# The softmax work of the later batches, cut into halves and spread over the steps of the main loop

## The chip, the cores and the metric

The kernel runs on one core of a Trainium2 chip. The metric is the device time of one execution in microseconds (us), the median of three runs. TensorE is called PE here, VectorE DVE, ScalarE ACT, GpSimd POOL and SyncE SP, as in the profile.

## What is computed

There are 8 batches, each with 8 heads, 576 tokens and 64 numbers a head. First 32 pack tokens attend to the keys and values of a batch; then the queries attend to the 32 packed results. What comes out, 4608 rows of 512 numbers, goes through a gated layer with 1536 inner columns.

```python
def sm_attn(qq, kk, vv):
    s = scale * np.matmul(qq, kk.transpose(0, 1, 3, 2))
    s = s - np.max(s, axis=-1, keepdims=True)
    a = np.exp(s)
    a = a / (np.sum(a, axis=-1, keepdims=True) + 1e-09)
    return np.matmul(a, vv)
p_packed = sm_attn(p, k, v)
attn = sm_attn(q, p_packed, p_packed)
# x: attn as rows of (token, head * 64)
g = x @ w_gate
silu = g * (1.0 / (1.0 + np.exp(-g)))
out = (silu * (x @ w_val)) @ w_out
```

## The kernel before

The packed result of a batch is multiplied with the weights of gate and value first (`m_part`, which leaves the high and low parts `mh` and `ml`), so that the second attention's weights (`a2h`, `a2l`) can be multiplied with that directly. Each operand of the large products is split into a rounded high part and a rest, and three products are summed.

The main loop runs over the batches b, and within one over 12 chunks of 128 inner columns (`fc`). In a chunk, `gv_chunk` makes the gate tile and the value tile for half A of the tokens (256 of them), then for half B (320). Each such half takes two PSUM banks of the tag `gv`, of which there are only two: the gate tile is read by the Silu on ACT (`sg`, L435), the value tile by `hf` and, for half B, by `t` as well (L438, L441, both on DVE). The next half's gate tile can be written once the Silu has read the last one, its value tile once `hf` and `t` have. `h_split` makes `hh` on ACT and `hl` on DVE; `out_mm` (L446), one chunk later, multiplies them with the output weights.

The attention of the next batch, d = b + 1, is made between these products: `aux_of(b)` is a generator, and `fill()` takes one step of it after every half chunk (from chunk 1 on; an `m_part` for the next two chunks stands in the odd chunks). PE's instructions stand in the order in which this code is written. The other engines' order is set by a scheduler that goes by the order of the code and by what depends on what; each engine then works through its own list from first to last. The products of the attention and of `m_part` use two PSUM banks of the tag `aux`; those of `m_part` come free when DVE has made `ml` (L85).

Batches 0 and 1 go over the older functions (`s1_...`); batches 2 to 7 take `q_scores` (L262), `q_weights` and `q_pack` (L325) for the pack tokens, where the tokens lie on the partitions by quarters and the heads by parity. In `q_weights` the sums over a quarter (L284) go to DRAM and come back for all four quarters (L287, L289); then follow the common factor (L295 to L306), the product of the weights with it (L307) and the transpositions (L312). All batches then take `s2_scores` (two groups of products, L164, and transpositions L348), `s2_max` (L363, L364), `s2_exp` (L368, on ACT), `s2_norm` (sum L375, L376, L377, scale L378) and `s2_back` (transposition L384 and the split into `a2h` and `a2l`). The argument `both` lets one instruction work on both halves of the tokens, 128x1152 numbers. The attention of batch 1 is made during batch 0, which keeps the values h of all chunks (`kept`, h0) and splits them only later; the output weights are converted there too (L101 to L105).

Of the kernel before, what the change touches and what calls it, by code (L numbers as in the profile page):

```python
# [15 lines left out]
ALU = mybir.AluOpType  # L16
AX = mybir.AxisListType
# [3 lines left out]
B, H, S, D = 8, 8, 576, 64  # L21
NP = 32
DM, DF = 512, 1536
P = 128
NPAR, NHP = 2, 4
NFC = DF // P
SC, NSC = 96, 6
NJ, SQ = 4, S // 4
# [13 lines left out]
def tile_pack_attention_swiglu(ctx: ExitStack, tc: tile.TileContext, qT, kT, v, vq, pT, wgv, wout, out):  # L42


    nc = tc.nc
# [37 lines left out]
    def split(dst_h, dst_l, src, hi=nc.scalar, lo=nc.vector):  # L83
        copy(hi, dst_h, src)
        lo.tensor_tensor(dst_l, src, dst_h.bitcast(F32), op=ALU.subtract)  # L85
# [52 lines left out]
    def load_k(b):  # L138
        p_t = pool.tile([P, NHP, NP], F32, tag="p", bufs=2, name="p_t")
        (nc.sync if b else nc.scalar).dma_start(p_t, pT[b])  # L140
        k_t = io_tile([P, 2, NHP, HS], F32, "k_t")
        for hf in range(2):
            nc.sync.dma_start(k_t[:, hf], kT[b, :, hf])
        kps[b] = (k_t, p_t)
# [21 lines left out]
    def s1_scores(b, direct):  # L166
        k_t, p_t = kps[b]
        t1 = pool.tile([P, NPAR, S], F32, tag="s2", bufs=1, name="t1")
        mx = pool.tile([P, NPAR, 2], F32, tag="mx1", bufs=2, name="mx1")
        nm = pool.tile([P, 2, NPAR], F32, tag="nm1", bufs=2, name="nm1")  # L170
        rs = pool.tile([P, 3, NPAR], F32, tag="rs1", bufs=3, name="rs1")
        st1[b] = [t1, rs, nm]
        kept = []
        for hf in range(2):
            pss = [ps(), ps()]
            kept.append(pss)
            by_head(
                [x[:, :HS] for x in pss], lambda r, hp: p_t[r, hp, :],
                lambda r, hp: k_t[r, hf, hp],
            )  # L180
            for par in range(NPAR):
                nc.vector.tensor_reduce(mx[:, par, hf : hf + 1], pss[par][:, :HS], axis=AX.X, op=ALU.max)
                if not direct:
                    nc.scalar.copy(t1[:, par, hf * HS : (hf + 1) * HS], pss[par][:, :HS])  # L184
            yield
        nc.vector.tensor_reduce(nm[:, 0], mx, axis=AX.X, op=ALU.max)
        nc.vector.tensor_scalar(nm[:, 1], nm[:, 0], -SCALE, None, op0=ALU.mult)
        if direct:
            for par in range(NPAR):
                for hf in range(2):  # L190
                    nc.scalar.activation(
                        t1[:, par, hf * HS : (hf + 1) * HS], kept[hf][par][:, :HS], AF.Exp,
                        bias=nm[:, 1, par : par + 1], scale=SCALE, accum_out=rs[:, 1 + hf, par : par + 1],
                    )
            nc.vector.tensor_tensor(rs[:, 0], rs[:, 1], rs[:, 2], op=ALU.add)

    def s1_exp(b):
        t1, rs, nm = st1[b]
        for par in range(NPAR):
            nc.scalar.activation(  # L200
                t1[:, par], t1[:, par], AF.Exp, bias=nm[:, 1, par : par + 1], scale=SCALE, accum_out=rs[:, 0, par : par + 1]
            )
# [74 lines left out]
    def q_weights(b):  # L277


        e, z = sq[b]  # L280
        ev = e.rearrange("p r h n -> p (r h) n")
        nc.scalar.activation(ev[:, :, :SQ], ev[:, :, :SQ], AF.Exp, scale=SCALE)
        zv = z.rearrange("p s r h -> p s (r h)")
        nc.vector.tensor_reduce(zv[:, 1], ev[:, :, :SQ], axis=AX.X, op=ALU.add)  # L284
        x = pool.tile([P, NJ, 2, H], F32, tag="x1", bufs=1, name="x1")
        zd = dram.tile([P, 2, H], F32, tag="zd", bufs=2, name="zd")
        nc.sync.dma_start(zd, zv)  # L287
        for i in range(NJ):
            nc.sync.dma_start(x[NP * i : NP * i + NP], zd.rearrange("(j n) s h -> n j s h", j=NJ))  # L289
        for _ in range(3):  # L290
            yield
        y = pool.tile([P, 3, NJ + 1, H], F32, tag="pp", bufs=1, name="y1")
        m, t, f = y[:, 2, 0], y[:, 2, 1], y[:, 2, 2]
        tc.keep_in_program_order(
            nc.vector.tensor_reduce(m, x[:, :, 0].rearrange("p j h -> p h j"), axis=AX.X, op=ALU.max)  # L295
        )
        nc.vector.tensor_tensor(
            y[:, 0, :NJ], x[:, :, 0], m.unsqueeze(1).broadcast_to([P, NJ, H]), op=ALU.subtract
        )
        nc.vector.tensor_tensor(y[:, 0, NJ], zv[:, 0], m, op=ALU.subtract)  # L300
        nc.scalar.activation(y[:, 0], y[:, 0], AF.Exp, scale=SCALE)
        nc.vector.tensor_tensor(y[:, 1, :NJ], y[:, 0, :NJ], x[:, :, 1], op=ALU.mult)
        nc.vector.tensor_reduce(t, y[:, 1, :NJ].rearrange("p j h -> p h j"), axis=AX.X, op=ALU.add)
        nc.vector.tensor_scalar(f, t, 1e-9, None, op0=ALU.add)
        nc.vector.reciprocal(t, f)
        nc.vector.tensor_tensor(f, t, y[:, 0, NJ], op=ALU.mult)  # L306
        nc.vector.tensor_tensor(  # L307
            ev[:, :, :SQ], ev[:, :, :SQ], f.unsqueeze(2).broadcast_to([P, H, SQ]), op=ALU.mult
        )
        a1 = pool.tile([P, NPAR, NHP, NKQ, NP], F32, tag="a1", bufs=1, name="a1")  # L310
        for par in range(NPAR):
            nc.vector.transpose(  # L312
                a1[:, par].rearrange("p h k n -> p (h k n)"), e[:, par].rearrange("p h n -> p (h n)")
            )
        sq[b] = a1
        for _ in range(2):
            yield

    def q_pack(b):
        a1, v_t = sq.pop(b), vs.pop(b)  # L320
# [11 lines left out]
    def s2_tiles(b):  # L332
        st2[b] = (
            pool.tile([P, 2, NPAR, HS], F32, tag="s2", bufs=1, name="s2"),
            pool.tile([P, 3, 2 * NPAR * NBK], F32, tag="r2", bufs=1, name="r2"),
        )
# [14 lines left out]
    def s2_view(b, cs):  # L351
        s2, r2 = st2[b]
        n = NPAR * NBK
        rows = slice(cs.start * n, cs.stop * n)
        return (
            s2[:, cs].rearrange("p c r (k n) -> p (c r k) n", n=NP),
            [r2[:, i, rows] for i in range(3)],
            [P, (cs.stop - cs.start) * n, NP],
        )

    def s2_max(b, cs):
        x, (m, _, _), shape = s2_view(b, cs)
        nc.vector.tensor_reduce(m, x, axis=AX.X, op=ALU.max)  # L363
        nc.vector.tensor_tensor(x, x, m.unsqueeze(2).broadcast_to(shape), op=ALU.subtract)  # L364
# [5 lines left out]
    def s2_a2(b):  # L370
        a2[b] = tuple(pool.tile([P, NPAR, S], F32R, tag=t, bufs=2, name=t) for t in ("a2h", "a2l"))

    def s2_norm(b, cs):
        x, (m, s, r), shape = s2_view(b, cs)
        nc.vector.tensor_reduce(s, x, axis=AX.X, op=ALU.add)  # L375
        nc.vector.tensor_scalar(m, s, 1e-9, None, op0=ALU.add)  # L376
        nc.vector.reciprocal(r, m)  # L377
        nc.vector.tensor_tensor(x, x, r.unsqueeze(2).broadcast_to(shape), op=ALU.mult)  # L378

    def s2_back(b, c):  # L380
        s2, _ = st2[b]
        ah, al = a2[b]
        t = pool.tile([P, NPAR, HS], F32, tag="t2", bufs=1, name="t2")
        nc.vector.transpose(t.rearrange("p r n -> p (r n)"), s2[:, c].rearrange("p r n -> p (r n)"))  # L384
        at = (slice(None), slice(None), slice(c * HS, (c + 1) * HS))
        split(ah[at], al[at], t)
# [72 lines left out]
    both = slice(0, 2)  # L459
# [6 lines left out]
    def aux_of(b):  # L466

        d = b + 1
        if d == B:
            return  # L470
        if d < NEARLY:
            yield from s1_scores(d, False)
            if d + 1 < B:
                load_k(d + 1)
            s1_exp(d)
            yield
            yield from s1_post(d)
        else:
            yield from q_scores(d)
            yield from q_weights(d)  # L480
            if d + 1 < B:
                load_k(d + 1)
            q_pack(d)
            yield
            yield
        if d + 1 < B:
            load_v(d + 1)
        s2_tiles(d)
        yield from s2_scores(d)
        if d + 1 < B:  # L490
            load_q(d + 1)
        s2_max(d, both)
        s2_exp(d, both)
        s2_norm(d, both)
        s2_a2(d)
        for c in range(2):
            s2_back(d, c)

    with tc.manual_schedule(engines={mybir.EngineType.PE}):

# [15 lines left out]
        for c in range(2):  # L516
            s2_max(0, slice(c, c + 1))
            s2_exp(0, slice(c, c + 1))
            if c == 0:
                m_part(0, 0, slice(0, 1))  # L520
            s2_norm(0, slice(c, c + 1))
            s2_back(0, c)
        load_w(3)
        load_k(1)
# [141 lines left out]
```

## Time and profile before

| what | us |
|---|---|
| median of the runs | 797.8 (797.77 to 798.69) |
| the profiled execution | 797.01 |
| its span | 795.2 |
| PE busy in it | 743.4 |
| DVE busy | 454.1 |
| ACT busy | 349.8 |
| POOL busy | 19.5 |

In the rows of the profile, L stands for a line of the code above, and an arrow for "written from". Rows in order of time begin with the start and the length in us; a bracket at the end tells for how long the engine sat idle just before and which instruction let it go on. In rows that group instructions, "x" is their count, and behind the bar stand the busy time in us and the mean length of one in ns. Rows of waits give the sum in us, the number of waits and the longest. The row of a stretch gives its length, then the busy us of PE, PE's weight loads, DVE, ACT and POOL with counts, then the granted TensorE clock, the share of the DMA engines and GB/s. A float32 product of the attention shows as two rows of PE. The ends of products are modelled, so that a wait of PE can also lie within the length of a row.

### The profile page before, as it was taken

To read this page: it belongs to the slowest core of one execution; us is meant where nothing else is said; L and a number is where in the kernel's file an instruction comes from. 1 tells how busy PE (TensorE), PEld (TensorE's weight loads), DVE (VectorE), ACT (ScalarE), POOL (GpSimd) and SP (SyncE) were. 2 spreads that over 40 slices of the span, in tenths; PEclk is the share of its full clock that TensorE was granted. 3 is DMA by queue.
4 is the path that set the end of the run, shared out by engine and by line. 5 is a ranking of instruction groups with operands and counts; after the bars stand their busy time and mean duration, and the time that the engine had idled before them with its cause. 6 is when DMAs were issued, how large, how long until landed. Compare 5 with 4: busy or idle time off the path is not lost.

```text
span 795.2 us, 14294 instructions
## 1 busy us (share of the span) xinstructions
PE 743.4 (93%) x5866; PEld 599.5 (75%) x5866; DVE 454.1 (57%) x968; ACT 349.8 (44%) x665; POOL 19.5 (2%) x25
## 2 busy tenths in 40 slices
PE   5579789999999999999999999999999999999998
PEld 3357567787788877878788777878778877888886
DVE  3998777455745656355745557455554556443434
ACT  3688664453532625354432445335442444343331
POOL 0001122000000000000000000000000000000000
PEclk9999998999999999999999999999999999999999
DMA  9957742221101230021101211010101000010001
GB/s 316 305 202 266 259 161 74 100 66 67 61 1 67 66 106 22 27 92 68 60 1 67 67 67 61 1 55 3 68 1 53 16 2 1 2 54 2 1 1 66
DMA packets 19776, 59.09 MB, mean 74 GB/s; under 512 B 5952, under 2 KB 6976, under 8 KB 17216
## 3 DMA queue, kind: packets, MB, share of 16 engines
q1 hardware_dynamic: 19568, 58.12, 20.9%
q8 instruction: 46, 0.75, 0.4%
q14 instruction: 18, 0.15, 0.1%
q10 hardware_dynamic: 144, 0.07, 0.0%
HBM read 48.69 MB, written 9.49 MB: 73 GB/s over the span
## 4 chain that ended last, share of the span: by engine, by line
PE 72%; DVE 15%; ACT 8%; DMA 2%; issue 2%; POOL 0%; SPq 0%; DVEq 0%; ACTq 0%
PE gv L428 31%; PE acc L446 27%; PE aux L164 6%; PE aux L446 4%; DVE ml L85 2%; PE aux L325 2%; DMA v_t<-in_v 2%; DVE r L375 1%; DVE s L378 1%; DVE r L363 1%; ACT L435 1%; DVE s L364 1%; DVE w L104 1%; PE aux L262 1%; DVE hf L438 1%
## 5 line engine op out<-in xcount | busy, mean ns | idle before, releaser
L428 PE MATMUL gv<-a2h,ml 128*128 128x256 f32 (+1 forms) x768 | 175.8, 311 | 28.4 <-DVE t L441 9.2
L428 PEld LDWEIGHTS gv<-a2h,ml 128*128 128x128 f32 x768 | 128.8, 191 | 65.6 <-issue 23.0
L428 PE MATMUL gv<-a2l,mh 128*128 128x256 f32 (+1 forms) x768 | 166.7, 299 | 0.9 <-DVE a2l L85 0.9
L428 PE MATMUL gv<-a2h,mh 128*128 128x256 f32 (+1 forms) x768 | 166.1, 298 | 0.0
L435 ACT ACTIVATE sg<-gv 128x256 f32<-128x256 f32 x192 | 78.8, 411 | 191.2 <-PE gv L428 140.0
L446 PE MATMUL acc<-wo_h,hl 128*128 128x512 f32 x384 | 157.0, 409 | 4.1 <-DVE hl L85 4.1
L438 DVE TENSOR_TENSOR hf<-gv,sg 128x256 f32<-128x256 f32 x168 | 71.1, 423 | 155.8 <-PE gv L428 153.1
L446 PE MATMUL acc<-wo_l,hh 128*128 128x512 f32 x384 | 151.8, 395 | 0.0
L446 PE MATMUL acc<-wo_h,hh 128*128 128x512 f32 x384 | 151.1, 394 | 0.0
L79 ACT CAST hh<-hf 128x256 fp32r<-128x256 f32 x168 | 68.1, 405 | 143.4 <-DVE hf L438 143.4
L428 PEld LDWEIGHTS gv<-a2l,mh 128*128 128x128 f32 x768 | 125.4, 192 | 1.5 <-DVE a2l L85 1.5
L428 PEld LDWEIGHTS gv<-a2h,mh 128*128 128x128 f32 x768 | 125.6, 192 | 0.0
L446 PEld LDWEIGHTS acc<-wo_h,hl 128*128 128x128 f32 x384 | 72.8, 189 | 51.1 <-issue 35.7
L85 DVE TENSOR_TENSOR hl<-hf,hh 128x256 fp32r<-128x256 f32 x168 | 70.4, 419 | 52.8 <-ACT hh L79 52.8
L446 PEld LDWEIGHTS acc<-wo_h,hh 128*128 128x128 f32 x384 | 72.7, 189 | 16.7
L446 PEld LDWEIGHTS acc<-wo_l,hh 128*128 128x128 f32 x384 | 72.9, 190 | 9.5
L85 DVE TENSOR_TENSOR ml<-aux,mh 128x512 fp32r<-128x512 f32 (+1 forms) x106 | 63.0, 630 | 13.1 <-ACT mh L79 12.9
L164 PE MATMUL aux<-w,ppt 64*32 64x512 f32 (+1 forms) x848 | 56.1, 564 | 4.2 <-ACT t L184 4.0
L79 ACT CAST mh<-aux 128x512 fp32r<-128x512 f32 (+1 forms) x106 | 52.2, 546 | 8.0 <-PE aux L164 2.9
L435 ACT ACT_TABLE_LOAD x21 | 26.9, 1283 | 0.7
L102 ACT ACTIVATE st<-st,minus_two 128x1024 f32<-128x1024 uint32 x18 | 22.4, 1246 | 0.6 <-DMA st<-in_wout 0.6
L164 PEld LDWEIGHTS aux<-w,ppt 64*32 64x32 f32 x848 | 10.4, 106 | 13.5 <-ACT t L184 5.0
(127 smaller groups left out, 591.2 us busy)
## 6 DMA issues: line engine op xcount, KB each, us to landing
st<-in_wgv SPq DMA_DIRECT2D x12, 1024.0 KB, 6.0
k_t<-in_kT SPq DMA_DIRECT2D x16, 576.0 KB, 4.9
q_t<-in_qT SPq DMA_DIRECT2D x16, 576.0 KB, 4.7
out<-ot SPq DMA_DIRECT2D x36, 256.0 KB, 2.1
v_t<-in_vq SPq DMA_DIRECT2D x6, 1280.0 KB, 5.7
st<-in_wout SPq DMA_DIRECT2D x6, 1024.0 KB, 6.1
v_t<-in_v SPq DMA_DIRECT2D x2, 1152.0 KB, 12.6
p_t<-in_pT SPq DMA_DIRECT2D x7, 64.0 KB, 3.0
```

The lines of the kernel that those rows point to most:

```text
L79: e.copy(dst, src)
L85: lo.tensor_tensor(dst_l, src, dst_h.bitcast(F32), op=ALU.subtract)
L102: nc.scalar.activation(lo.bitcast(F32), lo.bitcast(U32), AF.Identity, bias=minus_two, scale=LOW_WORD)
L104: nc.vector.scalar_tensor_tensor(d, d, 3, lo, op0=ALU.logical_shift_left, op1=ALU.bitwise_or)
L164: nc.tensor.matmul(outs[par][32 * hp : 32 * hp + 32], lhs(r, hp), rhs(r, hp), start=True, stop=True)
L262: nc.tensor.matmul(pss[par][NP * j : NP * j + NP, i * SQ : (i + 1) * SQ], p_t[r, 2 * g + i, :], k_t[r, j // 2, 2 * g + i, j % 2 * SQ : j % ...
L325: nc.tensor.matmul(p_p[D * par : D * par + D, NP * hp : NP * hp + NP], v_t[:, par, hp, k, :], a1[:, par, hp, k, :], start=(k == 0), stop=( ...
L363: nc.vector.tensor_reduce(m, x, axis=AX.X, op=ALU.max)
L428: nc.tensor.matmul(pg[:, :n], m_[:, g, f, s * P : (s + 1) * P], a_[:, g, off : off + n], start=(i == 0), stop=(i == 5),)
L435: nc.scalar.activation(sg[:, :n], pgs[0][:, :n], AF.Silu)
L438: nc.vector.tensor_tensor(hf, pgs[1][:, o : o + 256], sg[:, o : o + 256], op=ALU.mult)
L446: nc.tensor.matmul(acc[:, :], h_[:, c : c + P], w_[fc], start=(fc == 0 and i == 0), stop=(fc == NFC - 1 and i == 2),)
```

## The change

Three things are done, for the attentions that `aux_of` makes (batches 1 to 7; the first two only for batches 2 to 7):

- In `q_weights` the sum over the quarters and the product with the factor are made for each parity by itself, and each parity's product is followed at once by its transposition and a step.
- One of the two empty steps behind `q_pack` is gone, so that the scores of the queries come one step sooner. The number of steps ahead of `q_pack` stays.
- `s2_max`, and the sum and scale of `s2_norm` (now `s2_sums` and `s2_scale`), are called for each half of the tokens, with a step between; the exponential stays one instruction over both. `s2_back` has a step behind each half.

```diff
-        nc.vector.tensor_reduce(zv[:, 1], ev[:, :, :SQ], axis=AX.X, op=ALU.add)
+        for par in range(NPAR):
+            nc.vector.tensor_reduce(z[:, 1, par], e[:, par, :, :SQ], axis=AX.X, op=ALU.add)
...
-        nc.vector.tensor_tensor(
-            ev[:, :, :SQ], ev[:, :, :SQ], f.unsqueeze(2).broadcast_to([P, H, SQ]), op=ALU.mult
-        )
         a1 = pool.tile([P, NPAR, NHP, NKQ, NP], F32, tag="a1", bufs=1, name="a1")
         for par in range(NPAR):
+            w = e[:, par, :, :SQ]
+            nc.vector.tensor_tensor(
+                w, w, f[:, NHP * par : NHP * par + NHP].unsqueeze(2).broadcast_to([P, NHP, SQ]), op=ALU.mult
+            )
             nc.vector.transpose(
                 a1[:, par].rearrange("p h k n -> p (h k n)"), e[:, par].rearrange("p h n -> p (h n)")
             )
+            yield
         sq[b] = a1
-        for _ in range(2):
-            yield
...
-    def s2_norm(b, cs):
-        x, (m, s, r), shape = s2_view(b, cs)
+    def s2_sums(b, cs):
+        x, (m, s, r), _ = s2_view(b, cs)
         nc.vector.tensor_reduce(s, x, axis=AX.X, op=ALU.add)
         nc.vector.tensor_scalar(m, s, 1e-9, None, op0=ALU.add)
         nc.vector.reciprocal(r, m)
+
+    def s2_scale(b, cs):
+        x, (_, _, r), shape = s2_view(b, cs)
         nc.vector.tensor_tensor(x, x, r.unsqueeze(2).broadcast_to(shape), op=ALU.mult)
...
             q_pack(d)
             yield
-            yield
         if d + 1 < B:
             load_v(d + 1)
         s2_tiles(d)
         yield from s2_scores(d)
         if d + 1 < B:
             load_q(d + 1)
-        s2_max(d, both)
+        halves = [slice(c, c + 1) for c in range(2)]
+        for c in halves:
+            s2_max(d, c)
+            yield
         s2_exp(d, both)
-        s2_norm(d, both)
         s2_a2(d)
+        for c in halves:
+            s2_sums(d, c)
+            yield
+            s2_scale(d, c)
+            yield
         for c in range(2):
             s2_back(d, c)
+            yield
```

What this makes of the engines' lists is seen best in three places, the same in each of the batches 2 to 7 (shown for batch 2; line numbers of the new code differ by a few: L311 and L314 are the product and transposition of L307 and L312, L432 and L450 the products of L428 and L446, L439, L442 and L445 the Silu, `hf` and `t`, L369 the exponential, L331 the copy after `q_pack`). First DVE, where the weights of the pack tokens (e) are multiplied with the factor (y) and transposed into a. Before:

```order
L306 TENSOR_TENSOR y_1808<-y_1808 128x8
L307 TENSOR_TENSOR e_1593<-e_1593,y_1808 128x8x144
L438 TENSOR_TENSOR hf<-gv,sg 128x256
L312 STREAM_TRANSPOSE a_1819<-e_1593 128x640 x2
L85 TENSOR_TENSOR hl<-hf,hh 128x256
```

The same place on DVE after the change:

```order
L307 TENSOR_TENSOR y_1815<-y_1815 128x8
L311 TENSOR_TENSOR e_1599<-e_1599,y_1815 128x4x144 x2
L314 STREAM_TRANSPOSE a_1825<-e_1599 128x640
L442 TENSOR_TENSOR hf<-gv,sg 128x256
L314 STREAM_TRANSPOSE a_1825<-e_1599 128x640
L85 TENSOR_TENSOR hl<-hf,hh 128x256
```

One of the two transpositions now stands ahead of `hf`.

Next PE, from the `m_part` that follows `q_pack` (its products read the weights w and the packed result ppt). Before:

```order
L164 MATMUL aux<-w_84,ppt 32x512 x8
L446 MATMUL acc<-wo_h,hl 128x512
L446 MATMUL acc<-wo_l,hh 128x512
L446 MATMUL acc<-wo_h,hh 128x512
L446 MATMUL acc<-wo_h,hl 128x512
L446 MATMUL acc<-wo_l,hh 128x512
L446 MATMUL acc<-wo_h,hh 128x512
L428 MATMUL gv<-a2h,ml 128x320 x2
```

The same place on PE after the change:

```order
L164 MATMUL aux<-w_84,ppt 32x512 x8
L450 MATMUL acc<-wo_h,hl 128x512
L450 MATMUL acc<-wo_l,hh 128x512
L450 MATMUL acc<-wo_h,hh 128x512
L450 MATMUL acc<-wo_h,hl 128x512
L450 MATMUL acc<-wo_l,hh 128x512
L450 MATMUL acc<-wo_h,hh 128x512
L164 MATMUL aux<-q_t,ppt 32x288 x8
L432 MATMUL gv<-a2h,ml 128x320 x2
```

The first group of the queries' scores (q_t) now stands ahead of half B of this chunk; before, it stood behind that half, and the second group one half chunk later, as it does now behind the first.

Last ACT, around the exponential of the second attention (s). Before:

```order
L435 ACTIVATE sg<-gv 128x256
L368 ACT_TABLE_LOAD
L368 ACTIVATE s_2002<-s_2002 128x1152
L79 CAST mh<-aux 128x512 x2
L79 CAST hh<-hf 128x256
L435 ACT_TABLE_LOAD
L435 ACTIVATE sg<-gv 128x320
```

The same place on ACT after the change:

```order
L439 ACTIVATE sg<-gv 128x256
L79 CAST hh<-hf 128x256
L369 ACT_TABLE_LOAD
L369 ACTIVATE s_1981<-s_1981 128x1152
L439 ACT_TABLE_LOAD
L439 ACTIVATE sg<-gv 128x320
```

The exponential comes one chunk sooner: the two casts of `mh` now stand further down, and the Silu of half B follows the second table load at once.

More of the change, by code (lines that the diff above doesn't have):

```diff
@@ L520, in tile_pack_attention_swiglu @@
                 m_part(0, 0, slice(0, 1))
-            s2_norm(0, slice(c, c + 1))
+            s2_sums(0, slice(c, c + 1))
+            s2_scale(0, slice(c, c + 1))
             s2_back(0, c)
```

## The prediction

> **What bounds the kernel now.** I read the page first: the span, the busy shares, the chain that ended last. Then the waits of PE, and after that the stretch around each wait in order of time.
>
> ```profile
> span 795.2 us, 14294 instructions
> PE 743.4 (93%) x5866; PEld 599.5 (75%) x5866; DVE 454.1 (57%) x968; ACT 349.8 (44%) x665; POOL 19.5 (2%) x25
> PE 72%; DVE 15%; ACT 8%; DMA 2%; issue 2%; POOL 0%; SPq 0%; DVEq 0%; ACTq 0%
> ...
> PE gv L428 <- DVE t L441: 9.2, 6, 1.5
> PE acc L446 <- DVE hl L85: 4.1, 1, 4.1
> ```
>
> PE is busy for 93% of the span and holds 72% of the chain: it is the bound, and VectorE, at 57%, matters only where PE waits for it. Of those waits one comes again in each of six batches: 1.5 us for t of L441, 9.2 us in all. That is the most that a new order on VectorE can give back in the batches that it edits in full. The 4.1 us are the one long stall of the first batch. No VectorE work is taken away by the change, so everything hangs on which wait PE meets, and where.
>
> The six-fold stall, once, with the ACT, DVE and PE rows ahead of it:
>
> ```profile
> 387.33 1.28 ACT L368 ACT_TABLE_LOAD   x1
> 388.62 1.17 ACT L368 ACTIVATE s<-s 128x1152 f32<-128x1152 f32 x1
> 392.41 0.44 ACT L435 ACTIVATE sg<-gv 128x320 f32<-128x320 f32 x1
> ...
> 392.94 1.34 DVE L378 TENSOR_TENSOR s<-s,r 128x1152 f32<-128x1152 f32 x1
> 394.20 0.42 DVE L438 TENSOR_TENSOR hf<-gv,sg 128x256 f32<-128x256 f32 x1
> 395.22 0.18 DVE L441 TENSOR_TENSOR t<-gv,sg 128x64 f32<-128x64 f32 x1
> ...
> 395.55 0.47 PE L428 MATMUL gv<-a2h,ml 128*128 128x256 f32 x2 [1.54 <-DVE t L441]
> ```
>
> The gate was ready at 392.85, but hf and t, which free the PSUM bank of the value half, stood behind a product of 1.34 us over both halves of the tokens (L378), and t behind a transposition (L384) besides. PE restarts 0.14 us after t ends.
>
> **The change, part by part.** Three places in each of the batches 2 to 7, and the first stage.
>
> *Place A, the weights of the pack tokens, by parity.* The one product over both parities (L307) becomes two, and the transposition of the first parity now stands ahead of the next hf; before, hf stood between product and transpositions.
>
> ```profile
> 364.37 1.36 DVE L307 TENSOR_TENSOR e<-e,y 128x1152 f32<-128x1152 f32 x1
> 365.64 0.42 DVE L438 TENSOR_TENSOR hf<-gv,sg 128x256 f32<-128x256 f32 x1
> ...
> 365.66 0.46 PE L428 MATMUL gv<-a2h,mh 128*128 128x320 f32 x2
> 366.12 0.56 PE L428 MATMUL gv<-a2h,ml 128*128 128x320 f32 x2
> ...
> L378 DVE TENSOR_TENSOR s<-s,r 128x576 f32<-128x576 f32 x2 | 1.5, 748 | 0.0
> L312 DVE STREAM_TRANSPOSE a<-e 128x640 f32<-128x640 f32 x12 | 9.4, 818 | 0.0
> ...
> 355.43 2.79 SPq L289 DMA_DIRECT2D x<-zd  x4
> x<-zd SPq DMA_DIRECT2D x4, 8.0 KB, 2.8
> 362.05 0.20 DVE L295 TENSOR_REDUCE y<-x 128x8 f32<-128x32 f32 x1
> ```
>
> Hf ends at 366.06 and PE takes the freed bank at 366.12, so hf has no slack here already. A VectorE instruction that waits for nothing starts 0.09 us before the one ahead ends (365.64 against 365.73). With halves of 748 ns and a transposition of 818 ns: halves 364.37 and 365.03 to 365.78, transposition 365.69 to 366.51, hf 366.42 to 366.84. That is 0.78 us later, and PE with it: **+0.78 a batch**. The least is 0.6 (two halves no longer than the whole leave 0.73, and PE may come later by a tenth), the most 0.9. The sums (L284, now by parity) let an hl go between them, 0.4 us longer till both are done. Their trip over DRAM ends by 358.2 + 2.8 = 361.0 and L295 wants it at 362.05: the DMA's slack of 1.0 covers it; without this cover it would cost the 0.4.
>
> *Place B, the scores of the query tokens, half a chunk earlier.* One empty step after q_pack is gone, so the first group of scores comes right after the products that follow an m_part, and needs the two aux banks that this m_part filled; ml (L85) frees them.
>
> ```profile
> 374.46 1.29 DVE L85 TENSOR_TENSOR ml<-aux,mh 128x512 fp32r<-128x512 f32 x2 [0.30 <-ACT mh L79]
> ...
> 374.95 0.40 PE L446 MATMUL acc<-wo_h,hh 128*128 128x512 f32 x1
> 375.18 0.46 PE L428 MATMUL gv<-a2h,ml 128*128 128x320 f32 x2
> 378.09 0.40 PE L446 MATMUL acc<-wo_h,hh 128*128 128x512 f32 x1
> 378.42 0.71 PE L164 MATMUL aux<-q_t,ppt 64*32 64x288 f32 x16
> 379.07 0.50 PE L428 MATMUL gv<-a2h,ml 128*128 128x256 f32 x2
> ...
> 343.46 1.25 PE L262 MATMUL aux<-k_t,p_t 64*32 64x144 f32 x32
> 347.98 0.72 PE L262 MATMUL aux<-k_t,p_t 64*32 64x144 f32 x32
> ```
>
> The second ml ends at 375.75. PE would reach the scores at 375.27: 0.23 us lie between two products (374.95 to 375.18), 0.33 ahead of such a group (378.09 to 378.42). Their second product writes the other bank and can start at 375.75 + 0.14 = 375.89; the group takes 0.65 (378.42 to 379.07), nearly all of it after that: the next chunk starts at 376.5 in place of 375.18 + 0.75, the group's own time, which its old place gives back. That is +0.57. The scores of the pack tokens stand in just this position already, and their two groups differ by it: 1.25 against 0.72, 0.53 us. I take **+0.55**, bounds 0.3 (if only half of the wait shows) and 0.6. This wait hides in a row's length, not in a bracket.
>
> *Place C, the softmax by halves.* L378 and L384 leave the way of hf, so the 1.54 goes. What is late next is the gate: on ACT the exponential now stands ahead of the Silu of the B half of the chunk, with a table load on each side. Walk it from the second group of scores, which now stands where the first stood (378.42):
>
> ```profile
> 379.23 0.85 DVE L348 STREAM_TRANSPOSE s<-aux 128x288 f32<-128x288 f32 x2 [0.70 <-PE aux L164]
> 380.87 0.42 DVE L438 TENSOR_TENSOR hf<-gv,sg 128x256 f32<-128x256 f32 x1 [0.79 <-PE gv L428]
> ...
> 382.07 0.71 PE L164 MATMUL aux<-q_t,ppt 64*32 64x288 f32 x16
> 385.96 0.40 PE L428 MATMUL gv<-a2h,ml 128*128 128x256 f32 x2
> ```
>
> The maximum over the half runs 380.10 to 380.85 (748 ns), hf 380.87 to 381.29, the subtraction of the half 381.21 to 381.95. ACT then loads the table (1.28, to 383.26), takes the exponential of 1.17 (383.28 to 384.45), loads Silu's table (384.46 to 385.74) and runs the Silu to 386.19; PE can write the gate's bank at 386.33. Without the group at 382.07, PE asks for it at 385.96 - 0.75 = 385.21: a wait of 1.1. Hf and t follow the Silu, ending at about 386.9, in time for the value bank at 387.05. So **C gives 1.54 and takes 1.10: -0.44**. Bounds: -1.0 (chain half a us shorter), -0.2 (value bank waits as well).
>
> [...]
>
> *The first stage.* The batch-1 softmax runs among the h0 splits.
>
> ```profile
> 120.98 0.79 PE L446 MATMUL acc<-wo_h,hl 128*128 128x512 f32 x1 [4.08 <-DVE hl L85]
> 121.57 0.63 PE L446 MATMUL acc<-wo_l,hh 128*128 128x512 f32 x1
> 122.00 0.63 PE L446 MATMUL acc<-wo_h,hh 128*128 128x512 f32 x1
> ...
> 111.47 0.41 ACT L79 CAST hh<-h 128x256 fp32r<-128x256 f32 x1 [2.77 <-PE acc L446]
> 114.96 1.13 ACT L101 ACTIVATE wo_f<-st 128x1024 f32<-128x1024 f32 x1 [1.72 <-POOL wo_l L85]
> L104 DVE SCALAR_TENSOR_TENSOR wo_f<-wo_f,st 128x1024 int32<-128x1024 int32 x6 | 7.3, 1224 | 0.8 <-ACT st L102 0.7
> ...
> 118.90:125.70 6.80, 4.72 (x11) 3.75 (x12) 5.39 (x10) 2.70 (x5) 2.25 (x1) 0.50 0.50 173
> ```
>
> Before, five halves of h are multiplied, then PE waits for the sixth hl, till 120.98. Now only four are split ahead of the exponential, since the table load follows the fourth cast (to 111.88): load to 113.2, exponential to 114.35, both half sums to 115.8. The fifth hl stands behind L103 (0.7, after L101, which POOL holds as before), L104 and L105 (1.22 each) and a scale of 0.75: placed one behind the other, it ends at about 120.0. PE thus comes back 0.9 us sooner but six products behind, at half clock: the row's granted clock is 0.50, and products start 0.43 us apart from 121.57 to 122.00. Until 125.7 it does 13 products instead of 11 and stays 4 behind, 0.23 us each: **+0.9**. Bounds: +2.6, two of its later waits added (each of about a place's size), and -0.9, should the clock rise one window sooner.
>
> *Costed at nothing:* 28 more VectorE instructions: each split costs about 0.15 us (twice 748 ns against 1.34), in an engine that is idle for 43%; at A and C it is counted above. SP's and POOL's queues stand in the same order; v and q loads go out half a chunk sooner into buffers that were free.
>
> **Sum.** 0.78 + 0.55 - 0.44 = 0.89 a batch, times 6 = 5.3, plus 0.9 = **6.2 us**. The profiled execution took 797.01 us (span 795.2 and 1.8 around it): 803.2. The median of the runs is 797.8, 0.8 above it: **804.0**.
>
> **The rivals.**
> 1. *Not slower: the Silu comes in time.* If the load and the exponential start 1.1 us sooner at place C, the whole 1.54 is won. A batch then costs -0.21, in all -1.3 + 0.9: 797.4, no change. For it speaks that ACT is busy for 44% only; against it, four rows of fixed length in one queue. It decides at 385.21.
> 2. *The change does all it says:* hf isn't held at A either (if PE comes 0.8 us later there). Then 0.55 - 1.54, times 6, + 0.9 = -5.0: 792.8. Against it: PE takes that bank 0.06 us after hf.
> 3. *Slower still:* the value bank waits at C too and nothing is won there: 1.33 times 6 + 2.6 = 10.6: 808.4. For it: hf and t end only 0.1 us ahead of PE.
> 4. *The clock of the first stage rises one window (3.4 us, half of the 6.8 us at 0.50) sooner*, because PE idles less in it: eight products at full clock, -0.9 in place of +0.9: 802.2. [...]
>
> **How the numbers follow.** My forecast 0.67; rival 1 0.08, rival 2 0.04, rival 3 0.10, rival 4 0.11. About 0.2% (1.6 us) is what a measurement here can tell from no change. Slower: 0.67 + 0.10 + 0.11 = 0.88, less 0.03 for terms at their low ends: 0.85. Same: 0.08 less 0.02 below, plus 0.03: 0.09. Faster: 0.06. The ends of the bounds together give 796 to 808; not all lie at one end, so the range for 8 in 10 is 800.0 to 807.5, which holds forecast and rival 4.
>
> **What would show it.** Right: the 1.5 us waits of gv on t are gone; six waits of gv on ACT's Silu of about 1.1; waits on hf of 0.7 to 0.9 at A (part of them in a longer PE row); the first group of q_t scores 0.5 us longer than the second. Wrong: no bracket on the Silu, or hf ahead of the transposition without delay; or the first stage off by more than 2 us.

## The result, and the profile after

The changed kernel takes 802.76 us (median of four executions, 801.84 to 803.88), the kernel before, run beside it, 797.88 (797.77 to 798.69): a ratio of 1.006 with a 95% interval of 1.0042 to 1.0077. It is slower by 4.9 us, and the interval leaves 3.4 to 6.1; the forecast was 6.2 us. The profiled execution took 802.63 us.

The page and the waits of PE after the change (a row of waits: who waits for whom, sum in us, how many, the longest):

```profile
span 800.9 us, 14342 instructions
PE 747.2 (93%) x5866; PEld 599.9 (75%) x5866; DVE 457.6 (57%) x1022; ACT 351.8 (44%) x665; POOL 17.4 (2%) x25
...
PE gv L432 <- ACT sg L439: 10.6, 12, 1.9
PE gv L432 <- DVE hf L442: 4.9, 7, 0.8
PE acc L450 <- DVE hl L85: 4.4, 1, 4.4
```

The row for t, 9.2 us before, is gone. In its place stand six waits more on the Silu (12, of which six are those of the first stage) and six of 0.8 us on hf. The long stall of the first stage is 4.4 us instead of 4.1. VectorE's share of the span is 57% as before (1022 instructions instead of 968, 3.5 us more): nothing of the waits is to be seen in its busy time.

The three places in one batch, in order of time. First A, where the first transposition of the pack tokens' weights stands ahead of hf:

```profile
366.77 1.43 DVE L311 TENSOR_TENSOR e<-e,y 128x576 f32<-128x576 f32 x2
368.11 0.84 DVE L314 STREAM_TRANSPOSE a<-e 128x640 f32<-128x640 f32 x1
368.87 0.39 DVE L442 TENSOR_TENSOR hf<-gv,sg 128x256 f32<-128x256 f32 x1
369.31 0.56 PE L432 MATMUL gv<-a2h,ml 128*128 128x320 f32 x2 [0.79 <-DVE hf L442]
```

Then B, the two groups of the queries' scores. No bracket marks the wait; the first row is 0.54 us longer than the second:

```profile
378.46 1.25 PE L164 MATMUL aux<-q_t,ppt 64*32 64x288 f32 x16
...
382.98 0.71 PE L164 MATMUL aux<-q_t,ppt 64*32 64x288 f32 x16
```

And C, the exponential between its two table loads, the Silu behind them, and PE, which comes 0.05 us after the Silu's end at 390.82:

```profile
386.60 1.28 ACT L369 ACT_TABLE_LOAD   x1 [0.30 <-DVE s L365]
387.90 1.17 ACT L369 ACTIVATE s<-s 128x1152 f32<-128x1152 f32 x1
389.08 1.28 ACT L439 ACT_TABLE_LOAD   x1
390.38 0.44 ACT L439 ACTIVATE sg<-gv 128x320 f32<-128x320 f32 x1
390.87 0.50 PE L432 MATMUL gv<-a2h,ml 128*128 128x256 f32 x2 [1.01 <-ACT sg L439]
```

The six waits of this kind are 0.73, four of 1.01 or 1.02, and 1.07 us.

### The profile page after: what moved, and what is told of

Same layout as the page of the kernel before. It is cut to its first block, busy times and chain, and to the rows that moved or that the text cites. A ratio compares the mean times of both kernels' runs of the same rounds, so it can differ in the third digit from the quotient of the medians.

```text
span 800.9 us, 14342 instructions
## 1 busy us (share of the span) xinstructions
PE 747.2 (93%) x5866; PEld 599.9 (75%) x5866; DVE 457.6 (57%) x1022; ACT 351.8 (44%) x665; POOL 17.4 (2%) x25
## 4 chain that ended last, share of the span: by engine, by line
PE 76%; DVE 12%; ACT 8%; issue 2%; DMA 2%; SPq 0%; DVEq 0%; ACTq 0%
PE gv L432 32%; PE acc L450 29%; PE aux L164 7%; PE aux L450 4%; PE aux L326 2%; DMA v_t<-in_v 2%; DVE ml L85 1%; ACT L439 1%; DVE w L104 1%; PE aux L262 1%; ACT L369 1%; DVE hf L442 1%; ACT s L369 1%; ACT L302 1%; DVE s L349 1%
## 5 line engine op out<-in xcount | busy, mean ns | idle before, releaser
L432 PE MATMUL gv<-a2h,ml 128*128 128x256 f32 (+1 forms) x768 | 175.9, 311 | 29.7 <-ACT sg L439 10.6
L432 PEld LDWEIGHTS gv<-a2h,ml 128*128 128x128 f32 x768 | 128.3, 191 | 67.9 <-ACT sg L439 19.1
L432 PE MATMUL gv<-a2l,mh 128*128 128x256 f32 (+1 forms) x768 | 166.7, 299 | 0.9 <-DVE a2l L85 0.9
L432 PE MATMUL gv<-a2h,mh 128*128 128x256 f32 (+1 forms) x768 | 166.1, 298 | 0.0
L439 ACT ACTIVATE sg<-gv 128x256 f32<-128x256 f32 x192 | 79.0, 412 | 192.9 <-PE gv L432 144.1
L450 PE MATMUL acc<-wo_h,hl 128*128 128x512 f32 x384 | 157.0, 409 | 4.4 <-DVE hl L85 4.4
L442 DVE TENSOR_TENSOR hf<-gv,sg 128x256 f32<-128x256 f32 x168 | 70.5, 419 | 155.9 <-PE gv L432 153.5
L450 PE MATMUL acc<-wo_l,hh 128*128 128x512 f32 x384 | 152.0, 396 | 0.0
L450 PE MATMUL acc<-wo_h,hh 128*128 128x512 f32 x384 | 151.2, 394 | 0.0
L432 PEld LDWEIGHTS gv<-a2l,mh 128*128 128x128 f32 x768 | 125.2, 192 | 1.5 <-DVE a2l L85 1.5
L432 PEld LDWEIGHTS gv<-a2h,mh 128*128 128x128 f32 x768 | 125.6, 192 | 0.0
L450 PEld LDWEIGHTS acc<-wo_h,hl 128*128 128x128 f32 x384 | 72.9, 190 | 51.1 <-issue 35.7
L450 PEld LDWEIGHTS acc<-wo_h,hh 128*128 128x128 f32 x384 | 72.8, 190 | 16.8
L450 PEld LDWEIGHTS acc<-wo_l,hh 128*128 128x128 f32 x384 | 73.0, 190 | 9.6
L445 DVE TENSOR_TENSOR t<-gv,sg 128x64 f32<-128x64 f32 x96 | 20.6, 214 | 0.0
```

The costliest lines, as they stand in the source:

```text
L432: nc.tensor.matmul(pg[:, :n], m_[:, g, f, s * P : (s + 1) * P], a_[:, g, off : off + n], start=(i == 0), stop=(i == 5),)
L439: nc.scalar.activation(sg[:, :n], pgs[0][:, :n], AF.Silu)
L442: nc.vector.tensor_tensor(hf, pgs[1][:, o : o + 256], sg[:, o : o + 256], op=ALU.mult)
L445: nc.vector.tensor_tensor(t4[b // 2][:, fc, r], pgs[1][:, r4], sg[:, r4], op=ALU.mult)
L450: nc.tensor.matmul(acc[:, :], h_[:, c : c + P], w_[fc], start=(fc == 0 and i == 0), stop=(fc == NFC - 1 and i == 2),)
```

## The experiments

All medians are against the kernel before, with the ratio's 95% interval; beside the three sets of runs it took 797.88, 797.84 and 797.92 us. Line numbers move by a few between the kernels: L431, L432 and L434 are the same products, as are L438, L439 and L441 the Silu; the tiles' names tell which instruction a row shows.

### Place A undone

```diff
-        for par in range(NPAR):
-            nc.vector.tensor_reduce(z[:, 1, par], e[:, par, :, :SQ], ...)
+        nc.vector.tensor_reduce(zv[:, 1], ev[:, :, :SQ], ...)
...
+        nc.vector.tensor_tensor(ev[:, :, :SQ], ev[:, :, :SQ], f..., op=ALU.mult)
         for par in range(NPAR):
-            w = e[:, par, :, :SQ]
-            nc.vector.tensor_tensor(w, w, f[...]..., op=ALU.mult)
             nc.vector.transpose(a1[:, par]..., e[:, par]...)
-            yield
+        for _ in range(2):
+            yield
```

> The changed kernel with the weights of the pack tokens as they were (one sum, one product, both transpositions behind it, two steps). Theory: place A costs the 0.80 us that each of six batches now waits for hf, and nothing else takes it up: 802.8 - 4.8 = 798.0, the waits of gv on hf back to 0.2. Rival: the later wait on the Silu grows when PE comes sooner, since ACT's chain sets the pace there: 802.8, no change.

Measured: 798.07 us, ratio 1.0003 (0.9992 to 1.0014). The theory holds: 4.7 us come back, and the waits on hf are gone but for one of 0.2 us at the start of batch 1. The six later waits on the Silu have not grown (0.73 and five times 1.01 us); the row's larger sum comes from the first 100 us, where one wait took 2.27 us in place of 0.87:

```profile
PE gv L431 <- ACT sg L438: 11.9, 12, 2.3
...
PE gv L431 <- DVE hf L441: 0.2, 1, 0.2
```

### The transpositions a step later

This asks which part of A costs: that one product became two, or what stands ahead of hf.

```diff
             nc.vector.tensor_tensor(w, w, f[...]..., op=ALU.mult)
+        yield
+        for par in range(NPAR):
             nc.vector.transpose(a1[:, par]..., e[:, par]...)
-            yield
         sq[b] = a1
+        yield
```

> The changed kernel with the products by parity kept, but the step put between them and both transpositions, so that on DVE hf stands behind two products and ahead of both transpositions. Theory: it is the transposition of 0.84 us ahead of hf that costs, not the cut of the product: the two halves take 1.43 where the one product took 1.36, so a wait of at most 0.1 is left and 0.80 x 6 goes: 798.0 to 798.6. Rival: the cut itself costs (more instructions, sums by parity): 801 to 803.

Measured: 798.1 us, ratio 1.0 (0.999 to 1.001). Two products ahead of hf leave 0.07 us of the 0.79: from the start of the row ahead of the wait to the row behind it PE takes 0.52 us here, and 0.45 with place A undone. The cut itself is nearly free; the one transposition of 0.84 us that moved ahead of hf is what A costs.

### The empty step put back

```diff
             q_pack(d)
             yield
+            yield
```

> The changed kernel with the empty step behind q_pack put back, so that the scores of the queries come half a chunk later again. Theory: the 0.54 us on the aux bank go (-3.2), and the wait on the Silu as well (-6.1): half a chunk later the exponential stands ahead of the Silu of an A half, behind which the products of an m_part (8 pairs of two rows) lie before PE asks for the gate's bank again. 793.6, with the waits on hf at A left at 0.80. Rival: the wait on the Silu belongs to the softmax by halves and only moves half a chunk on: 799.6.

Measured: 792.3 us, ratio 0.9931 (0.9914 to 0.9948), so 10.5 us less than the changed kernel, a little more than the 9.3 expected. Both groups of scores are short now, and of the waits on the Silu only the six of the first stage are left:

```profile
290.19 0.71 PE L164 MATMUL aux<-q_t,ppt 64*32 64x288 f32 x16
293.85 0.72 PE L164 MATMUL aux<-q_t,ppt 64*32 64x288 f32 x16
...
PE gv L432 <- DVE hf L442: 4.9, 7, 0.8
...
PE gv L432 <- ACT sg L439: 4.8, 6, 2.0
```

So the wait on the Silu does not come with the softmax by halves alone: without the half chunk by which the scores were moved it is not there. Whether it needs the halves as well is seen where place C is undone, below.

### The exponential behind the Silu, the scores still early

The step of the experiment before takes two waits away at once. This one tells them apart: the scores stay early, and the exponential alone is held behind what ACT had been given when it is written.

```diff
-        nc.scalar.activation(x, x, AF.Exp, scale=SCALE)
+        i = nc.scalar.activation(x, x, AF.Exp, scale=SCALE)
+        if b >= NEARLY:
+            tc.keep_in_program_order(i)
...
             s2_max(d, c)
-            yield
+            if c.start == 0 or d < NEARLY:
+                yield
         s2_exp(d, both)
+        if d >= NEARLY:
+            yield
```

> The changed kernel, with the exponential of the queries' scores (batches 2 to 7) held on ACT behind the Silu and the cast of the B half that it stood ahead of; the scores keep their early place. It tells the wait on the Silu from the wait on the aux bank, which came and went together when the empty step was put back (-10.5 measured, -9.3 by the rows). Theory: the wait on the Silu goes (six times 1.0, -6.1), since the next gate tile is asked for only after an m_part; the 0.54 on the aux bank and the 0.80 on hf stay: 796.7. Rival: ACT is late for the A half then, or the later sums push a wait into the next chunk: 800 or more.

Measured: 796.37 us, ratio 0.9982 (0.9973 to 0.9991). The wait on the Silu goes, the long row of B and the waits on hf stay:

```profile
289.95 0.13 PEld L164 LDWEIGHTS aux<-q_t,ppt 64*32 64x32 f32 x2 [0.36 <-DVE ml L85]
289.95 1.25 PE L164 MATMUL aux<-q_t,ppt 64*32 64x288 f32 x16
290.48 0.18 PEld L164 LDWEIGHTS aux<-q_t,ppt 64*32 64x32 f32 x14 [0.40 <-DVE ml L85]
...
302.23 1.16 ACT L369 ACTIVATE s<-s 128x1152 f32<-128x1152 f32 x1
302.69 1.09 PE L164 MATMUL aux<-w,ppt 64*32 64x512 f32 x16
303.41 1.28 ACT L441 ACT_TABLE_LOAD   x1
304.71 0.39 ACT L441 ACTIVATE sg<-gv 128x256 f32<-128x256 f32 x1
305.14 0.30 PEld L434 LDWEIGHTS gv<-a2h,ml 128*128 128x128 f32 x2 [0.21 <-ACT sg L441]
```

The weight loads name what the products' row hides: ml, twice. And the Silu after the exponential, which ends at 305.10, is just in time, since the m_part at 302.69 and its output products lie ahead of the next gate tile: the weight load waits for it, but the product starts at 305.21, 0.24 us after the last one, as usual.

### Place C undone

```diff
-        for c in halves:
-            s2_max(d, c)
-            yield
+        s2_max(d, both)
         s2_exp(d, both)
-        s2_a2(d)
-        for c in halves:
-            s2_sums(d, c)
-            yield
-            s2_scale(d, c)
-            yield
+        s2_sums(d, both)
+        s2_scale(d, both)
+        s2_a2(d)
         for c in range(2):
             s2_back(d, c)
-            yield
```

> The changed kernel with maximum, sum and scale over both halves again and no steps in the softmax, in all batches. Theory that the places simply add: the wait on the Silu goes (-6.1), the 1.54 on t comes back (+9.2), the first stage gives 0.7 back: 805.2. Rival: a wait's size goes by where in the half chunk the work lands, and the scores now come half a chunk sooner than in the kernel before: a wait on t of about 0.9 in place of 1.5, and 801.

Measured: 801.17 us, ratio 1.0042 (1.0028 to 1.0056): the theory that the places simply add falls, the rival's 801 holds. The wait on t comes back at half of its old size:

```profile
PE gv L432 <- DVE hf L442: 5.0, 7, 0.8
...
PE gv L432 <- DVE t L445: 4.5, 6, 0.8
PE gv L432 <- ACT sg L439: 4.3, 6, 1.8
```

The six waits on the Silu that are left all lie in the first 100 us; none comes in the batches 2 to 7, though the scores are still early. So that wait takes both: the early scores and the softmax by halves. Either one undone removes it.

Half a chunk sooner, the same whole scale and transposition meet hf and t elsewhere, and PE waits 0.8 us for t in place of 1.5. What these long VectorE instructions cost is not their own: here it went by the place in the half chunk where their inputs come ready.

### A and B undone, the halves kept

The edits of the first and the third experiment together.

> Places A and B both undone; only the softmax of the queries by halves is left. Theory: all three waits go, 0.80 + 0.54 + 1.0 in six batches: 802.8 - 14.0 = 788.8, which is 9 us below the kernel before (its wait of 1.54 on t, six times, and nothing in its place). Rival: the gains don't add, since the wait on the Silu comes back when PE arrives sooner: 794 to 798.

Measured: 787.57 us, ratio 0.9872 (0.9854 to 0.9891). All three waits are gone and nothing has come for them; the gains of undoing A (4.7) and B (10.5) add to the 15.2 measured. The softmax by halves alone is thus worth 10.3 us against the kernel before, though that kernel's brackets on t came to 9.2 only.

### The halves for batches 2 to 7 only

```diff
+        if d < NEARLY:
+            s2_max(d, both)
+            ...
+            return
         for c in halves:
```

> Only the softmax of the queries by halves, as in the run with places A and B undone (787.6), and that only for batches 2 to 7: the attention of batch 1 goes as in the kernel before. Theory: the first stage gives its 0.7 back: 786.9, the stall on hl at 4.1 in place of 4.4, and POOL's rows beside VectorE's long again. Rival: the 0.7 was within what single traces differ by in that stage: 787.6.

Measured: 787.34 us, ratio 0.9863 (0.9849 to 0.9878). The stall is back at 4.1 us, but 0.2 us of difference between the medians tells neither theory. The first stage is taken up again below.

### One step more ahead of the pack tokens' scores

```diff
+            yield
             yield from q_scores(d)
...
             q_pack(d)
             yield
-            yield
```

and the weights of the pack tokens as in the run with the transpositions a step later.

> The run before it, with one empty step more ahead of the pack tokens' scores and one less behind q_pack, and their weights multiplied by parity with both transpositions a step later. The first group of the pack tokens' scores has the same long row as place B (1.25 against 0.72 for the second), in the kernel before too. Theory: away from the m_part it loses the 0.53, six times: -3.2 to 783.7, if nothing else comes. Rival: half a chunk later the product with the factor stands ahead of hf and t of a B half, and q_pack right behind an m_part, which costs a wait of 0.3 to 0.6 each: 785 to 788.

Measured: 784.94 us, ratio 0.983 (0.9813 to 0.9847), the fastest of all, 13 us below the kernel before. It lies between the two expectations: both groups of the pack tokens' scores take 0.72 us now, and two waits are new, on t and, ahead of q_pack's products, on ml:

```profile
258.60 0.72 PE L262 MATMUL aux<-k_t,p_t 64*32 64x144 f32 x32
262.25 0.72 PE L262 MATMUL aux<-k_t,p_t 64*32 64x144 f32 x32
...
280.63 0.48 PE L434 MATMUL gv<-a2h,ml 128*128 128x256 f32 x2 [0.41 <-DVE t L447]
...
284.31 2.41 PEld L328 LDWEIGHTS aux<-a,v_t 128*64 128x64 f32 x80 [0.56 <-DVE ml L85]
```

By the distances between the starts of products, summed over the six batches, the new waits take 3.4 and 1.2 us, more than the 3.2 that the scores give. What makes this kernel faster all the same went unforeseen: in the run before it two short waits without a bracket stand at the weights of the pack tokens, on the Silu (PE goes from 274.78 to 275.22, 0.44 us where 0.23 is usual) and on hf (275.92 to 276.37, 0.45 where 0.29 is usual). Neither is there now; with the rows behind them they came to 3.1 us. That adds up to 1.7 of the 2.0 us by which the two profiles differ from batch 1 on (the last column of the next table).

### Both kernels once more, for the first stage

Take three marks from each profile: the first product of the h0 halves into acc, the first m_part of batch 1, the last product. For the kernel before and after:

```profile
109.78 0.50 PE L446 MATMUL acc<-wo_h,hl 128*128 128x512 f32 x1
147.01 1.09 PE L164 MATMUL aux<-w,ppt 64*32 64x512 f32 x16
790.97 0.39 PE L446 MATMUL aux<-wo_h,hh 128*128 128x512 f32 x1
```

```profile
110.08 0.50 PE L450 MATMUL acc<-wo_h,hl 128*128 128x512 f32 x1
147.96 1.09 PE L164 MATMUL aux<-w,ppt 64*32 64x512 f32 x16
796.60 0.39 PE L450 MATMUL aux<-wo_h,hh 128*128 128x512 f32 x1
```

> The changed kernel, unchanged, for a second profile of its first stage. Five runs with the same order of batch 0 on every engine fall into two groups there, from the first product of the h0 halves to the m_part of batch 1: 37.8 to 37.9 us with two windows of half clock (6.8 us), 36.5 to 36.6 with one (3.4 us). Theory: it isn't the program that sets which, but where the stall of 4.4 us falls against the clock's windows in one execution; so this profile shows one of those two values and none between, and if 36.5, then in a program that took 37.88 before. Rival: the length goes with the program: 37.88 again, here and at each repeat.

> The kernel before, unchanged, for a second profile of its first stage, which took 37.24 us with two windows of half clock. Theory: 37.2 with two windows or 36.6 with one, as in the run that has its order of batch 0 and place A as after the change; so the first stage differs between the kernels by 0.6 at like clock with two windows, by nothing with one, and by up to 1.3 either way otherwise. Rival: 37.24 whatever the execution.

Each of the two is a single execution: 801.05 us after, 799.54 before. All twelve profiles by these marks (starts of the rows), with the length at half clock that begins around the stall on hl, and with how much of that stall is left when it begins (a minus: it begins after the stall):

| kernel | first stage, us | half clock, us | stall left, us | from m_part of batch 1 on, us |
|---|---|---|---|---|
| before | 37.23 | 6.8 | 2.09 | 643.96 |
| before, again | 37.41 | 6.8 | 1.58 | 643.55 |
| halves for batches 2 to 7 only | 37.21 | 6.8 | 2.05 | 633.15 |
| one step more | 37.46 | 6.8 | 1.02 | 631.18 |
| place C undone | 36.59 | 3.4 | -0.88 | 647.22 |
| after | 37.88 | 6.8 | 0.98 | 648.64 |
| after, again | 36.50 | 3.4 | 0.54 | 648.36 |
| place A undone | 36.50 | 3.4 | 0.48 | 643.74 |
| transpositions later | 36.57 | 3.4 | 0.37 | 644.22 |
| empty step put back | 37.88 | 6.8 | 0.89 | 637.78 |
| A and B undone | 37.85 | 6.8 | 1.07 | 632.98 |
| exponential behind the Silu | 37.93 | 6.8 | 0.85 | 641.38 |

In the first five rows batch 0 goes in the old order, in the other seven in the new one. The theory holds for the changed kernel: the same program took 37.88 us in one execution and 36.50 in another. The stretch in both (PE's clock is the third number from the end):

```profile
119.26:126.09 6.83, 5.85 (x14) 4.65 (x15) 5.35 (x12) 2.70 (x5) 1.43 (x2) 0.50 0.52 173
```

```profile
119.85:123.20 3.35, 2.89 (x7) 2.31 (x8) 2.62 (x8) 1.29 (x2) 0.00 (x0) 0.50 0.68 196
```

For the kernel before itself both profiles show the longer stretch; that its order can have the shorter one too is shown by the run with C undone. At equal clock the new order costs 0.4 to 0.7 us there with the longer stretch and nothing with the shorter. The longer stretch costs the new order 1.3 to 1.4 us.

In the clock record of the first profile of each of the two kernels, the stretches at half clock are 3.41, 3.41 and 6.83 us long, and those at full clock between them 34.13 and 17.07: whole multiples of 3.41. A last one at half clock, where the program ends, is 2.51 us long before and 0.94 after. In the 3.41 us ahead of each of the first three, PE was busy for 1.31, 1.41 and 1.42 us before, and for 1.25, 1.48 and 0.00 after.

What goes with 3.41 us or twice that is to be seen in the column on the stall. With 0.85 us or more of it left, the stretch is the longer one (eight profiles); with 0.54 or less, the shorter one (four). The first of the two stretches above begins at 119.26 and PE comes back at 120.24; the second begins at 119.77, a little ahead of its row, and PE comes back at 120.31. That what is left of the stall brings on the second 3.41 us is argued from these twelve profiles, in both orders; no run moved the stall alone. Where a stall falls against the stretches changes from one execution to the next: 0.98 and 0.54 us of it were left in the changed kernel, 2.09 and 1.58 in the kernel before.

## Why the prediction was right, point by point

From the m_part of batch 1 on, the change costs 648.64 - 643.96 = 4.7 us, or 0.78 a batch. The runs give each part by itself, from the last column and over six batches. Two profiles of one kernel differ there by 0.3 to 0.4 us, which is 0.07 a batch:

- **A: +0.78 forecast, +0.82 measured** (648.64 - 643.74 = 4.9). The transposition ahead of hf was the cause, as the walk through VectorE had it; the bracket is 0.79. The sums by parity, which are still there in the run with the transpositions later, cost nothing that its 798.1 us would show.
- **B: +0.55 forecast, +0.60 measured** (641.38 - 637.78 = 3.6: two kernels without the wait on the Silu, with the early scores and without; the first group's own row gives 0.53 of it, the row behind it 0.06). That the row of the pack tokens' scores already showed this price in the trace of before was the right reading.
- **C: -0.44 forecast, -0.62 measured.** The new wait was put at 1.10 and has a bracket of 1.01; taking it away gives 1.21 (648.64 - 641.38 = 7.3). The old one was put at its bracket of 1.54, and taking it away gives 1.83 (643.96 - 632.98 = 11.0). By the second profiles of both kernels these are 1.16 and 1.76, and by the medians 1.07 (6.4 us) and 1.76 (10.6 us, the run with the halves for batches 2 to 7 only). So it is mainly the old wait, in every reading above its bracket, that was mis-sized, and it is why the batches cost 4.7 us in place of 5.3. The forecast called 9.2 us the most that the old wait could give back; the profiles give 10.4 to 11.0. The new wait is booked at C here as in the forecast, but it takes B and C together.
- **The first stage: +0.9 forecast, +0.65 in the two profiles**, which have the same stretch at half clock by luck. PE came back at 120.24 instead of 120.98, 0.74 sooner, where 0.9 was forecast (1.04 sooner when counted from the first acc product). The stretch was as long as before in that profile, so rival 4 did not happen in it; in the second profile of the changed kernel it did, with -0.9 us against the second one of the kernel before. That rival's reason, PE idling less, was the author's estimate: the column on the stall speaks for it, and no run shows it alone. The forecast should have made this a matter of the execution, not of the change. A median holds an unknown mix of the two, so how near the measured 4.9 comes to the 6.2 is in part luck as well.
- **From profile to median** the forecast added 0.8 us. The profiles differ by 5.6 us and the medians by 4.9: that was noise of single executions. The kernel before started its first acc product at 109.78 us in one profile and at 112.54 in the other.
- **The count of VectorE's instructions** was wrong: 28 more were forecast, and it is 54 (968 to 1022). That they cost nothing by themselves holds for the 42 of C: they are still there with A and B undone (1010), and PE has no bracket of a wait in the batches 2 to 7 of that run.

The rivals by the experiments: rival 1 (the Silu in time) is what the exponential held behind the Silu brings about, 6.4 us less than the changed kernel, a little under the forecast's 6.6. Rival 2 (hf not held at A) fell with the brackets of 0.79 and 0.80. Rival 3's wait on the value bank never showed. At place C next to nothing lies between a table load and what follows it, before the change as after: the load that starts at 387.33 for 1.28 us is followed by the exponential at 388.62, and the one at 386.60 for 1.28 us by the exponential at 387.90.

Why does a wait cost more than its bracket? The rows around the old stall, of the kernel before:

```profile
393.38 0.40 PE L428 MATMUL gv<-a2l,mh 128*128 128x256 f32 x2
393.62 0.40 PE L428 MATMUL gv<-a2h,mh 128*128 128x256 f32 x2
395.55 0.47 PE L428 MATMUL gv<-a2h,ml 128*128 128x256 f32 x2 [1.54 <-DVE t L441]
395.87 0.40 PE L428 MATMUL gv<-a2l,mh 128*128 128x256 f32 x2
```

The bracket counts from the end of a row (394.02), but rows overlap: without a wait the next one starts 0.24 us after the last, here 1.93 after. That is 1.69, and the row behind a wait takes 0.32 instead of 0.24 till its successor. Together 1.77, near the 1.73 to 1.83 that the profiles of the two kernels with the halves alone and the two of the kernel before give.

A short wait can also have no bracket on the products: with A undone, PE goes from 366.85 to 367.30 at that place, 0.45 where 0.29 is usual for products of 320 columns. Only the row of the weight load says that it waited for hf.

```profile
366.85 0.46 PE L431 MATMUL gv<-a2h,mh 128*128 128x320 f32 x2
367.30 0.30 PEld L431 LDWEIGHTS gv<-a2h,ml 128*128 128x128 f32 x2 [0.26 <-DVE hf L441]
367.30 0.56 PE L431 MATMUL gv<-a2h,ml 128*128 128x320 f32 x2
```

## What to carry to other kernels

Where work for the next batch is slipped between the products of this one, cutting it into smaller pieces helps or hurts by what then stands ahead of the few instructions that free a bank (here hf, t, ml and the Silu), so walk each queue from the input that comes last to the instruction that PE waits for. Try the parts of such a change one by one: here one part is worth 10.3 us, and two that came along with it cost 15. That price holds only beside the halves: on the whole softmax the same two cost 3.3 us (801.17 against 797.84). To price a wait, take the distance between the starts of the products around it less the usual distance, and look for waits without a bracket in rows that are longer than their like and in the rows of the weight loads.

## What the runs showed of the hardware that was not expected

In the first stage, some rows of VectorE and POOL are longer where the two engines work at the same time. The old order, then the new one, with the same instructions hl and wo_l:

```profile
112.42 1.35 DVE L364 TENSOR_TENSOR s<-s,r 128x1152 f32<-128x1152 f32 x1
112.59 2.34 POOL L85 TENSOR_TENSOR wo_l<-wo_f,wo_h 128x512 fp32r<-128x512 f32 x1 [3.62 <-DVE hl L85]
113.69 1.51 DVE L85 TENSOR_TENSOR hl<-h,hh 128x256 fp32r<-128x256 f32 x1
```

```profile
112.59 0.42 DVE L85 TENSOR_TENSOR hl<-h,hh 128x256 fp32r<-128x256 f32 x1
113.09 1.30 POOL L85 TENSOR_TENSOR wo_l<-wo_f,wo_h 128x512 fp32r<-128x512 f32 x1 [3.83 <-DVE hl L85]
```

POOL's wo_l takes 2.34 us in place of 1.30 when it starts inside L364, and hl, which starts while POOL works, 1.51 in place of 0.42, ending 0.27 us after POOL does (114.93). L364 itself is not longer (1.35). These lengths come again to 0.01 us in all runs with the old order of batch 0, and wo_l took 1.29 or 1.30 at this place in all with the new one. What makes the rows long is not shown. Not every VectorE instruction goes with a long row: in the changed kernel a transposition that runs from 124.15 beside a wo_l from 124.31 takes 0.77 us and the wo_l 1.29, both as usual. Nor is it the old order's alone: in the changed kernel too an hl that starts at 138.21, while a wo_l from 137.95 works, takes 1.30. No cost of it can be seen here: at equal clock the stage with these long rows is the shorter or takes as long.
